# Trainium2: the first step of the later transforms on sums and differences of opposite rows, with 32x32 parts of the array

## The chip, the cores and the metric

One core of one Trainium2 chip. The core has TensorE (PE, 128x128 matmul array, with its weight loads shown apart as PEld), VectorE (DVE), ScalarE (ACT), GpSimd (POOL) and SyncE (SP), which mostly issues DMAs. Each engine works through its own queue in order and waits on semaphores of the others. The metric is the device time of one execution in microseconds (us), as the median of several.

## The reference

```python
X = np.fft.rfft(x, axis=1)                  # x: 8 batches, 3008 positions, 256 channels
F = (filt_r + 1j * filt_i)[None, :, :]      # one filter for all batches
y = np.fft.irfft(X * F, n=x.shape[1], axis=1)
x = y.reshape(8 * 3008, 256)                # 24064 tokens
g = x @ w_gate                              # 256 x 1536
return (g / (1 + np.exp(-g)) * (x @ w_val)) @ w_out     # 1536 x 256
```

All in float32. Along the positions each channel is filtered in the frequency domain; then each token goes through a gated feed-forward block (FFN).

## The kernel before

The FFN is most of the work. It runs batch by batch, and each batch in 12 steps (four chunks of tokens by three thirds of the hidden width). While batch b's FFN runs, the transform of batch b+1 is done in pieces between its products. The first transforms (batches 0 and 1) are done by other code. From the third batch on, that is during b = 1 to 6, the transform of batch b+1 has these pieces: in steps 0 to 3 its first step, `quads(0)` to `quads(3)`; in steps 4 to 10 `fours(...)`, which go on from the result; in step 11 nothing. In b = 7 there is nothing left to transform.

The order of all instructions is written out by hand: `SCHEDULE` is one list of tokens for a step, run through once per step, and `pin` keeps what is emitted in that order. A token names an operation of the FFN or a slot for transform work. `P`, `Q`, `A`, `B`, `E` with digits are products (`product`, L1075, 26 of them, two matmuls each), `W` and `o` the second matmuls of the FFN (L1172). The small letters before two digits are the operations around a product: `x03` makes an operand (L1097), `s13` another (L1097, written to the `wa` operand), which A13 multiplies; `c1` is a copy from PSUM by ScalarE (L1094), `y01`, `m13` and so on follow. `t` tokens call the transform's last step for other chunks. `b0` to `b7` each advance the step's iterator in `bursts` by one `yield`. The part of the order around them:

```python
"Q0 o3' z1.o' t4.2' W2 b0 f0 S00' S01' i0 b1 b2 x0.o' t0.0 x1.o' i1 Q1 t0.1 x2.o' P3 x3.o' f1 t4.3'"
"W1 x4.o' S10' x03 S11' D01 i2 i3 i4 s13 b3 x5.o' P1 o1 b4 t0.2 P0 o2 z0.o c1 i5 A13 g1 c0 S20' Q2"
...
" ... h2 b5 Q3 t2.1 h01 e12 A02 y23 W4 e02 b6 y03 m02 g3 ... l12 b7 E02 u12 ..."
```

**The first step before.** The 3008 positions are 47 rows (N1) of 64 (N2). `quads(g)` treats two pieces u = 2g and 2g+1, each of four neighbouring positions in each half of a row, 47 rows by 1024 numbers in each half of the partitions. At b0 eight matmuls (L716) multiply the 47 rows by a table of cosines and negated sines (47x64, the 48 outputs being 24 frequencies by real and imaginary part) on four 64x64 parts of the array. Each fp32 matmul is recorded as two passes. At b1 and b2, per piece, ScalarE copies one PSUM bank (L725), and VectorE subtracts and adds the other (L331 and L328, called from L726 and L727). At b3 and b4 ScalarE issues two stores each (L733) of 48 rows to the batch's `d1` tile in DRAM, and SyncE loads the x of a later piece (`load_x(u + 2)`, L618 as the helper's line). `load_four` (L743) reads `d1` back after step 3.

x is loaded into a shared SBUF tile `lent`, of which `room_of(name)` hands out places; a burst's tables, intermediate values and the filter's temporary share it. The x of the next batch's first two pieces is asked for in step 11, at Q2 and B01. In b = 1, steps 0 to 3, SyncE also carries the rearranging of the filter (`keep_filter` and `negated_filter`).

Of the kernel before, what the change touches and what calls it, by code (L numbers as in the profile page):

```python
# [41 lines left out]
FP32 = mybir.dt.float32  # L42
# [6 lines left out]
B, S, C = 8, 3008, 256  # L49
# [4 lines left out]
N1, N2 = 47, 64  # L54
NS, NQ = 24, 64
# [70 lines left out]
def dft_tables():  # L126
# [37 lines left out]
            if n >= NH:  # L164
                back[row:row + rows, first + N1 * i:first + N1 * (i + 1)] = one_hi[a:a + rows]

    quad = np.zeros((128, 64))
    for h, turn in enumerate((ph, ph + 2 * np.pi * s / (2 * N1))):
        cols = np.stack([np.cos(turn), -np.sin(turn)], 2).reshape(N1, 2 * NS)
        quad[64 * h:64 * h + N1, 0:2 * NS] = cols  # L170

    four = np.zeros((128, N_FOUR + 1, 2, 4, 64))
    lo, qq = np.arange(32), np.arange(32)
# [32 lines left out]
def kernel(  # L206
# [60 lines left out]
    def weights_of(b, k, g):  # L267
        return wt_1 if b == 0 and k < NT and g == 1 else wt_t

    dram_tiles = [wdpool.tile([2 * NS, N2, C], FP32, name=f"d{1 + i % 2}_{i // 2}")  # L270
                  for i in range(4)]
    yt_dram = [wdpool.tile([128, 3 * len(PAIRS), TQ], FP32, name=f"yt_{k}") for k in range(NT)]
    y_dram = [wdpool.tile([128, 8, TQ], FP32, name=f"y_{k}") for k in range(NCHUNK)]
    o_dram = [wdpool.tile([128, 4 * NH, RP], FP32, name=f"o_{k}") for k in range(NT)]
# [39 lines left out]

    def negated_filter(w, stage):

        t = room_of("et"[w % 2])[0:64].rearrange("p (s c) -> p s c", c=C)
        if stage == 0:
            for q in range(4):
                pin(nc.sync.dma_start(out=t[16 * q:16 * q + 16],  # L320
                                      in_=filter_rows(1, q // 2, q % 2, 4 * w, 4)))
        elif stage == 1:
            pin(nc.scalar.mul(t, t, -1.0))
        else:
            pin(nc.sync.dma_start(out=f_pairs[:, 0, 1, 4 * w:4 * w + 4], in_=t))
# [274 lines left out]
    class Spectral:  # L600


        def __init__(self, b):
            self.b = b
            self.d1, self.d2 = [dram_tiles[2 * (b % 2) + i] for i in range(2)]
# [23 lines left out]
        def load_x(self, u):  # L629
            if self.b == 0:  # L630
                rows = x[0].rearrange("(r n) c -> r n c", n=32)
                for a, n in ((0, 4), (4, 4)):
                    for r in (slice(0, 80), slice(80, NR)):
                        self.load(out=x0[u][r, a:a + n, :],
                                  in_=rows[r, 8 * u + a:8 * u + a + n, :])
            elif self.b > 1:
                if u < N_QUAD:
                    self.x[u] = room_of("x", u).rearrange("p (n c) -> p n c", c=C)
                    rows = x[self.b].rearrange("(r n) c -> r n c", n=N2)
                    for h in range(2):  # L640
                        for a, e in ((0, 32), (32, N1)):
                            self.load(out=self.x[u][64 * h + a:64 * h + e],
                                      in_=rows[a:e, 32 * h + 4 * u:32 * h + 4 * u + 4])
            elif u < N_ONE:
                self.x[u] = xpool.tile([NR, NV, C], FP32, name=f"x_{self.b}_{u}", tag="x")
                rows = x[self.b].rearrange("(r n) c -> r n c", n=32)

                for r in (slice(0, 80), slice(80, NR)):
                    self.load(out=self.x[u][r], in_=rows[r, ts(u, NV), :])
# [49 lines left out]
        def bank(self, name):  # L699
# [2 lines left out]
                return bank(name).rearrange("p (i c) -> p i c", i=NV)  # L702
            return fbank(name)

        def quads(self, g):

            pieces = (2 * g, 2 * g + 1)
            banks = {}
            for u in pieces:
                xt = self.x.pop(u)  # L710
                for h in range(2):
                    banks[u, h] = bank(f"qa_{self.b}_{u}_{h}")
                for cp in range(2):
                    for h in range(2):
                        r = slice(64 * h, 64 * h + N1)
                        pin(nc.tensor.matmul(  # L716
                            out=banks[u, h][64 * cp:64 * cp + 64], lhsT=quad_t[0][r, 0:64],
                            rhs=xt[r, 2 * cp:2 * cp + 2].rearrange("p n c -> p (n c)"),
                            start=True, stop=True))
            yield  # L720
            t1 = {u: room_of("yg"[i]).rearrange("p (n h c) -> p n h c", h=2, c=C)
                  for i, u in enumerate(pieces)}
            for u in pieces:
                low, high = [banks[u, h].rearrange("p (n c) -> p n c", c=C) for h in range(2)]
                pin(nc.scalar.copy(out=t1[u][:, :, 0], in_=low))  # L725
# [3 lines left out]
            d1 = self.d1.rearrange("a (n h) c -> a n h c", h=2)  # L729
            for u in pieces:  # L730
                for cp in range(2):
                    n = 4 * u + 2 * cp
                    pin(nc.scalar.dma_start(out=d1[:, n:n + 2], in_=t1[u][64 * cp:64 * cp + 2 * NS]))  # L733
                self.load_x(u + 2)
                yield
            if g == 3:
                self.load_filter(0)
                self.load_turns(0)
            yield
            if g == 3:  # L740
                self.load_four(0)

        def load_four(self, w):  # L743

            if w < N_FOUR:
                t = self.t2[w] = room_of("t").rearrange("p (s h c) -> p s h c", h=2, c=C)
                d1 = self.d1.rearrange("(s r) (n h) c -> s (r n) (h c)", r=2, h=2)
# [633 lines left out]
    for b in range(B):  # L1381
# [10 lines left out]
        if b and nxt:  # L1392
            for n in range(N_QUAD // 2):
                bursts[n] = nxt.quads(n)
            for n in range(N_FOUR + 1):
                bursts[N_QUAD // 2 + n] = nxt.fours(n)
        bursts = [iter(p) for p in bursts]
        two = []
        for u in range(N_TWO + 2) if b == 0 else ():
# [18 lines left out]
        for step in range(NCHUNK * NG + (b == B - 1)):  # L1418
# [16 lines left out]
            for place, token in enumerate(SCHEDULE):  # L1435
# [31 lines left out]
                    continue  # L1467
                if b == 0 and (step, op) == (5, "A23"):
                    nxt.load_two(0)
                if b + 2 < B and (step, op) in ((11, "Q2"), (11, "B01")):  # L1470
                    following.load_x(int(op == "B01"))
                if b == 1 and step < 4 and op in FILTER_AT:
                    n = FILTER_AT.index(op)
                    if n < 4 and step < 3:
# [48 lines left out]
```

## Time and profile before

| | us |
|---|---|
| median of 3 runs | 2821.73 |
| the runs | 2825.27, 2821.73, 2821.25 |
| the profiled execution | 2823.7 |
| its span, first to last instruction | 2821.6 |

The mean granted clock of TensorE over the span is 0.997 of full speed. The profile is of one execution, so sums made from its durations stand against 2823.7.

| group | busy, us |
|---|---|
| L1075 products, operand `wa` (x4464) | 881.6 |
| L1075 products, operand `wk` (x2976) | 572.0 |
| L1172 second matmuls, `wA` (x1532) | 551.8 |
| L1075 products, operand `we` (x2232) | 431.7 |

How to read it: "busy" of an engine is the sum of its instructions; matmuls are pipelined, so several can be in flight and a busy PE isn't one at its peak. "idle before" is time in which an engine stood before an instruction of the group, with what ended it. The chain of waits follows the work that ended last back to what released it. In names such as `wqa<-lent,quad` the output stands left of the arrow. DMA moved 586.59 MB in the span, 208 GB/s in the mean.

### The profile page before, as it was taken

Reading aid. Unit: us, or ns where it says so; the run is one execution under the profiler, and the core shown is the slowest. Engines: PE = TensorE matmul, PEld = TensorE weight load, DVE = VectorE, ACT = ScalarE, POOL = GpSimd, SP = SyncE. Lnnn points to the kernel's source line nnn. Section 1 sums busy time; section 2 is a strip of 40 time slices with the busy share of each in tenths; the row PEclk is TensorE's granted clock in tenths of the full one; section 3 lists DMA queues with packets and bytes.
Section 4 is the critical chain, followed back from the end, with each engine's and each line's share of the span. In section 5 each row is a group of like instructions: output and inputs, shape, how many; then the busy total and the mean of one; then the engine's idle time right before and its main releaser. Section 6 shows DMA issues by size and latency. Waiting matters only on the chain.

```text
span 2821.6 us, 48540 instructions
## 1 busy us (share of the span) xinstructions
PE 2787.5 (99%) x15444; PEld 2319.9 (82%) x15444; DVE 1999.1 (71%) x4579; ACT 1564.7 (55%) x4176; POOL 1579.9 (56%) x1689
## 2 busy tenths in 40 slices
PE   8999999999999999999999999999999999999998
PEld 6877888888888888788888888878888888888887
DVE  7898767767667766667766677667676767666666
ACT  5675455555555555555555555555555555555554
POOL 4786576465545565456653566445655455545544
PEclk9999999999999999999999999999999999999999
DMA  9687876877666775667666676667766677654443
GB/s 214 224 272 237 283 242 211 285 233 232 181 188 207 246 221 175 204 215 229 222 185 197 211 246 201 188 190 236 228 205 181 213 224 227 192 153 148 153 137 82
DMA packets 362933, 586.59 MB, mean 208 GB/s; under 512 B 198620, under 2 KB 245660, under 8 KB 362536
## 3 DMA queue, kind: packets, MB, share of 16 engines
q1 hardware_dynamic: 337722, 533.61, 60.8%
q10 hardware_dynamic: 22318, 44.38, 5.7%
q0 software_dynamic: 2640, 5.51, 0.7%
q8 instruction: 125, 2.05, 0.3%
q14 instruction: 128, 1.05, 0.1%
HBM read 467.48 MB, written 101.34 MB: 202 GB/s over the span
## 4 chain that ended last, share of the span: by engine, by line
PE 91%; POOL 2%; DVE 2%; DMA 1%; issue 1%; ACT 1%; ACTq 0%; SPq 0%; POOLq 0%; DVEq 0%
PE wa L1075 25%; PE wk L1075 17%; PE wA L1172 16%; PE we L1075 13%; PE wG L1172 8%; PE wF L1172 4%; PE pd L978 3%; PE wqa L716 2%; PE wqc L775 1%; PE wqb L787 1%; POOL out_dram L1157 0%; POOL h L331 0%; PE pa L857 0%; DMA lent<-later_tbl 0%; PE pd L981 0%
## 5 line engine op out<-in xcount | busy, mean ns | idle before, releaser
L1075 PE MATMUL wa<-y_t,wt_t 128*128 128x188 f32 x4464 | 881.6, 324 | 4.0 <-DVE wa L1097 2.3
L1075 PEld LDWEIGHTS wa<-y_t,wt_t 128*128 128x128 f32 x4464 | 749.8, 191 | 79.5 <-ACT wa L1101 9.3
L1075 PEld LDWEIGHTS wk<-y,wt_t 128*128 128x128 f32 x2976 | 495.0, 190 | 109.5 <-issue 33.4
L1075 PE MATMUL wk<-y,wt_t 128*128 128x188 f32 x2976 | 572.0, 325 | 3.2 <-ACT f L1090 3.2
L331 POOL TENSOR_TENSOR h<-h 128x376 f32<-128x376 f32 x572 | 559.6, 1000 | 15.4 <-DVE h L328 15.2
L328 POOL TENSOR_TENSOR h<-h 128x376 f32<-128x376 f32 x190 | 182.8, 983 | 685.5 <-DVE h L1122 685.5
L1172 PE MATMUL wA<-h,wo_t 128*128 128x376 f32 x1532 | 551.8, 482 | 3.9 <-DVE o L328 2.1
L1075 PE MATMUL we<-y_t,wt_t 128*128 128x188 f32 x2232 | 431.7, 323 | 1.6 <-ACT we L1106 1.5
L331 POOL TENSOR_TENSOR D<-f,f 128x376 f32<-128x376 f32 x288 | 280.0, 986 | 258.4 <-ACT f L1090 256.0
L331 DVE TENSOR_TENSOR we<-we,m 128x376 f32<-128x376 f32 x576 | 319.8, 556 | 141.1 <-PE we L1075 73.9
L1075 PEld LDWEIGHTS we<-y_t,wt_t 128*128 128x128 f32 x2232 | 369.3, 190 | 2.7 <-ACT we L1106 2.1
L1172 PEld LDWEIGHTS wA<-h,wo_t 128*128 128x128 f32 x1532 | 274.9, 190 | 113.7 <-issue 7.0
L1110 ACT COPY m<-wa 128x376 f32<-128x376 f32 x576 | 272.7, 473 | 102.0 <-PE wa L1075 98.8
L335 DVE SCALAR_TENSOR_TENSOR y<-wk,c 128x376 f32<-128x376 f32 x480 | 244.8, 541 | 63.8 <-ACT c L1094 37.8
L1117 ACT ACTIVATE g<-wa 128x188 f32<-128x188 f32 x576 | 187.5, 326 | 164.7 <-PE wa L1075 154.9
L1117 ACT ACTIVATE u<-we 128x188 f32<-128x188 f32 x576 | 188.7, 328 | 160.2 <-DVE we L331 153.3
L1172 PE MATMUL wG<-h,wo_t 128*128 128x376 f32 x768 | 274.0, 479 | 0.0
L1094 ACT COPY c<-wk 128x376 f32<-128x376 f32 x288 | 136.5, 474 | 226.0 <-PE wk L1075 196.7
L1090 ACT ACTIVATE f<-wk 128x376 f32<-128x376 f32 x288 | 140.4, 488 | 168.6 <-PE wk L1075 118.0
L1106 ACT COPY we<-y 128x376 f32<-128x376 f32 x480 | 222.3, 480 | 19.8 <-DVE h L1122 14.4
L1122 DVE TENSOR_TENSOR h<-wa,g 128x188 f32<-128x188 f32 x576 | 199.4, 347 | 38.0 <-ACT g L1117 37.6
L1122 DVE TENSOR_TENSOR h<-we,u 128x188 f32<-128x188 f32 x576 | 198.5, 345 | 28.8 <-ACT u L1117 17.3
(193 smaller groups left out, 3523.0 us busy)
## 6 DMA issues: line engine op xcount, KB each, us to landing
wt_t<-w_all SPq DMA_DIRECT2D x174, 896.0 KB
wt_t<-w_all SPq DMA_DIRECT2D x174, 768.0 KB
lent<-filter SPq DMA_DIRECT2D x36, 1024.0 KB
lent<-d SPq DMA_DIRECT2D x84, 256.0 KB
d<-lent ACTq DMA_DIRECT2D x84, 256.0 KB
d<-lent ACTq DMA_DIRECT2D x96, 192.0 KB
lent<-raw SPq DMA_DIRECT2D x144, 128.0 KB
t<-d SPq DMA_DIRECT2D x114, 128.0 KB
```

The source lines that it names most:

```text
L328: return eng.tensor_tensor(out=dst, in0=a, in1=b, op=ALU.add)
L331: return eng.tensor_tensor(out=dst, in0=a, in1=b, op=ALU.subtract)
L335: return nc.vector.scalar_tensor_tensor(out=dst, in0=a, scalar=-1.0, in1=b, op0=ALU.mult, op1=ALU.subtract)
L978: pin(nc.tensor.matmul(out=rows, lhsT=self.t4[k, i][:, j, ts(cb, 128)], rhs=cols, start=j == 0, stop=True, skip_group_check=True))
L1075: pin(nc.tensor.matmul(out=ps[:, z], lhsT=self.wt[:, SLOT[p], z], rhs=rhs, start=start and z == 0, stop=True, skip_group_check=True))
L1090: pin(act.mul(self.small(f"f{i}", f"f{i}", 1), t[f"k{i}"], -1.0))
L1094: pin(act.copy(out=self.small(f"c{i}", f"c{i}", 1), in_=t[f"k{i}"]))
L1106: pin(act.copy(out=self.bank(f"e{at}"), in_=t[f"y{at}"]))
L1110: pin(act.copy(out=self.small(f"m{at}", "m", 4), in_=t[f"a{at}"]))
L1117: pin(act.activation(out=self.small(op, "g", 3, 1)[:, 0], in_=ps[:, 1], func=AF.Silu))
L1122: pin(v.tensor_tensor(out=dst, in0=ps[:, 0], in1=g, op=ALU.mult))
L1172: pin(nc.tensor.matmul(out=self.tiles[at], lhsT=wo_t[:, JB * q + i, WO[p], :], rhs=self.hs[i][:, HID[p]], start=start and i == 0, stop=Tru ...
```

## The change

The row of the sum over 47 rows that lies at the same distance on the other side of the middle has the same cosine, and a sine of opposite sign. The change makes sums and differences of such opposite rows before the matmul, and multiplies the sums by cosines and the differences by sines alone, on 32x32 parts of the array. 47 rows become 24 sums and 24 differences, of which the middle row is met by itself (cosine halved, sine zero).

- New in every step that precedes a `quads`: `fold(g)`, four VectorE operations of 128x512 in SBUF, at b4, b5, b6 and b7, two sums into place `e` and two differences into place `t`. For the first step, `first_fold` does it in step 11 of the batch before.
- `quads(g)`: pieces g and g+4 instead of 2g and 2g+1; 16 matmuls of 24 rows by 32 columns by 512 instead of 8. Copies, subtractions and additions stay.
- Stores are of 64 rows instead of 48, to DRAM tiles of their own (`quads_dram`), and `load_four` reads these.
- x: six loads per fold (64, 23, 23, 2, 64 and 64 rows of 4 KB) instead of four per piece; a batch has 24 instead of 32. They are issued after the last operation of the fold before (b7), and for the first fold at Q0 of step 11.
- The temporary of `negated_filter` moves to the last two places of the shared tile.

Lines of the changed kernel lie 35 to 41 further down around the transform's code.

```diff
-    quad = np.zeros((128, 64))
-    for h, turn in enumerate((ph, ph + 2 * np.pi * s / (2 * N1))):
-        cols = np.stack([np.cos(turn), -np.sin(turn)], 2).reshape(N1, 2 * NS)
-        quad[64 * h:64 * h + N1, 0:2 * NS] = cols
+    quad = np.zeros((4, 32, 2, 32))
+    for h in range(2):
+        turn = 2 * np.pi * (np.outer(2 * np.abs(23 - 23 * h - n1[0:NS]) + h, s) % (2 * N1)) / (2 * N1)
+        quad[2 * h:2 * h + 2, 0:NS, 0, 0:NS], quad[2 * h:2 * h + 2, 0:NS, 1, 0:NS] = np.cos(turn), -np.sin(turn)
+        quad[2 * h:2 * h + 2, 23] *= np.array([0.5, 0.0])[:, None]
+    quad = quad.reshape(128, 64)
...
+    quads_dram = [wdpool.tile([64, N2, C], FP32, name=f"quads_{i}") for i in range(2)]
...
-        t = room_of("et"[w % 2])[0:64].rearrange("p (s c) -> p s c", c=C)
+        t = lent[64 * (w % 2):64 * (w % 2) + 64, 12 * NV * C:14 * NV * C]
+        t = t.rearrange("p (s c) -> p s c", c=C)
...
-                if u < N_QUAD:
-                    self.x[u] = room_of("x", u).rearrange("p (n c) -> p n c", c=C)
-                    rows = x[self.b].rearrange("(r n) c -> r n c", n=N2)
-                    for h in range(2):
-                        for a, e in ((0, 32), (32, N1)):
-                            self.load(out=self.x[u][64 * h + a:64 * h + e],
-                                      in_=rows[a:e, 32 * h + 4 * u:32 * h + 4 * u + 4])
+                if u < N_QUAD // 2:
+                    self.x[u] = [room_of("x", n) for n in range(2)]
+                    up, down = self.x[u]
...
+                    self.load(out=up[0:64], in_=rows(0, NS - 1, -1, ("i", 2), ("p", 32)))
+                    for i in range(2):
+                        self.load(out=down[32 * i:32 * i + NS - 1],
+                                  in_=rows(0, NS, 1, ("p", NS - 1), i=i))
+                    self.load(out=down[NS - 1:64:32], in_=rows(0, 0, 1, ("i", 2)))
+                    self.load(out=up[64:128], in_=rows(1, 0, 1, ("i", 2), ("p", 32)))
+                    self.load(out=down[64:128], in_=rows(1, N1 - 1, -1, ("i", 2), ("p", 32)))
...
+        def fold(self, g):
+
+            if g < N_QUAD // 2:
+                up, down = self.x.pop(g)
+                self.x[g] = [room_of("e"), room_of("t")]
+                for t, f in zip(self.x[g], (add, sub)):
+                    for half in range(2):
+                        a = ts(half, NV * C)
+                        pin(f(nc.vector, t[:, a], up[:, a], down[:, a]))
+                        if t is self.x[g][1] and half:
+                            self.load_x(g + 1)
+                        yield
+
+        def first_fold(self):
+
+            for _ in range(4):
+                yield
+            yield from self.fold(0)
...
-            pieces = (2 * g, 2 * g + 1)
-            banks = {}
-            for u in pieces:
-                xt = self.x.pop(u)
-                for h in range(2):
-                    banks[u, h] = bank(f"qa_{self.b}_{u}_{h}")
-                for cp in range(2):
-                    for h in range(2):
-                        r = slice(64 * h, 64 * h + N1)
-                        pin(nc.tensor.matmul(
-                            out=banks[u, h][64 * cp:64 * cp + 64], lhsT=quad_t[0][r, 0:64],
-                            rhs=xt[r, 2 * cp:2 * cp + 2].rearrange("p n c -> p (n c)"),
-                            start=True, stop=True))
-            yield
+            pieces = (g, g + N_QUAD // 2)
+            banks = {(u, h): bank(f"qa_{self.b}_{u}_{h}") for u in pieces for h in range(2)}
+            parts = self.x.pop(g)
+            for cp in range(2):
+                for t in range(2):
+                    for i, u in enumerate(pieces):
+                        for h in range(2):
+                            r, c = 32 * (2 * h + i), 32 * (2 * cp + t)
+                            pin(nc.tensor.matmul(
+                                out=banks[u, h][c:c + 32], lhsT=quad_t[0][r:r + NS, ts(t, 32)],
+                                rhs=parts[t][r:r + NS, ts(cp, NV * C)],
+                                start=True, stop=True))
+            yield
+            fold = self.fold(g + 1)
...
-                    pin(nc.scalar.dma_start(out=d1[:, n:n + 2], in_=t1[u][64 * cp:64 * cp + 2 * NS]))
-                self.load_x(u + 2)
+                    pin(nc.scalar.dma_start(out=d1[:, :, n:n + 2], in_=t1[u][64 * cp:64 * cp + 64]))
+                if u == pieces[1]:
+                    next(fold, None)
                 yield
             if g == 3:
                 self.load_filter(0)
                 self.load_turns(0)
+            next(fold, None)
             yield
             if g == 3:
                 self.load_four(0)
+            next(fold, None)
+            yield
+            next(fold, None)
...
+        if b + 2 < B:
+            bursts[-1] = following.first_fold()
...
-                if b + 2 < B and (step, op) in ((11, "Q2"), (11, "B01")):
-                    following.load_x(int(op == "B01"))
+                if b + 2 < B and (step, op) == (11, "Q0"):
+                    following.load_x(0)
```

More of the change, by code (lines that the diff above doesn't have):

```diff
@@ L604, in __init__ @@
             self.b = b
+            self.quads_dram = quads_dram[b % 2]
             self.d1, self.d2 = [dram_tiles[2 * (b % 2) + i] for i in range(2)]
@@ L636, in load_x, with rows @@
             elif self.b > 1:
-                if u < N_QUAD:
-                    self.x[u] = room_of("x", u).rearrange("p (n c) -> p n c", c=C)
-                    rows = x[self.b].rearrange("(r n) c -> r n c", n=N2)
-                    for h in range(2):
-                        for a, e in ((0, 32), (32, N1)):
-                            self.load(out=self.x[u][64 * h + a:64 * h + e],
-                                      in_=rows[a:e, 32 * h + 4 * u:32 * h + 4 * u + 4])
+                if u < N_QUAD // 2:
+                    self.x[u] = [room_of("x", n) for n in range(2)]
+                    up, down = self.x[u]
+                    xb = x[self.b]
+                    def rows(h, first, step, *dims, i=0):
+                        at = (N2 * first + 32 * h + 4 * u + 16 * i) * C
+                        ap = [[{"i": 16, "p": step * N2}[d] * C, n] for d, n in dims]
+                        return bass.AP(tensor=xb.tensor, offset=xb.offset + at,
+                                       ap=ap + [[1, 4 * C]])
+                    self.load(out=up[0:64], in_=rows(0, NS - 1, -1, ("i", 2), ("p", 32)))
[5 more added lines that the diff above has]
+                    self.load(out=down[64:128], in_=rows(1, N1 - 1, -1, ("i", 2), ("p", 32)))
             elif u < N_ONE:
@@ L728, in quads @@
                 yield
-            d1 = self.d1.rearrange("a (n h) c -> a n h c", h=2)
+            d1 = self.quads_dram.rearrange("(s t) (n h) c -> t s n (h c)", t=2, h=2)
             for u in pieces:
@@ L746, in load_four @@
                 t = self.t2[w] = room_of("t").rearrange("p (s h c) -> p s h c", h=2, c=C)
-                d1 = self.d1.rearrange("(s r) (n h) c -> s (r n) (h c)", r=2, h=2)
+                d1 = self.quads_dram.rearrange("(s r) (n h) c -> s (r n) (h c)", r=2, h=2)
                 for p in range(2):
```

## The prediction

> **What bounds the kernel now.** I read the page's busy times and chain first, then the groups by line, then one step's timeline. All in microseconds.
>
> ```profile
> PE 2787.5 (99%) x15444; PEld 2319.9 (82%) x15444; DVE 1999.1 (71%) x4579; ACT 1564.7 (55%) x4176; POOL 1579.9 (56%) x1689
> ...
> PE 91%; POOL 2%; DVE 2%; DMA 1%; issue 1%; ACT 1%; ACTq 0%; SPq 0%; POOLq 0%; DVEq 0%
> ```
>
> TensorE (PE) sets the end. A microsecond taken from it is worth a microsecond only where its next work is ready; the other engines have room on average, so only their lateness at one place can count. The rows of the burst that changes, and (last) the nearest row for the operation that is added, columns busy, mean ns of one, idle before:
>
> ```profile
> L716 PE MATMUL wqa<-lent,quad 47*64 47x512 f32 x384 | 46.7, 602 | 0.0
> ...
> L328 DVE TENSOR_TENSOR lent<-lent,wqa 128x512 f32<-128x512 f32 x48 | 33.0, 687 | 1.7
> L331 DVE TENSOR_TENSOR lent<-lent,wqa 128x512 f32<-128x512 f32 x48 | 32.8, 684 | 68.4 <-ACT lent L725 62.4 <-DMA t<-d 6.0
> ...
> L725 ACT COPY lent<-wqa 128x512 f32<-128x512 f32 x48 | 28.1, 586 | 47.0 <-PE wqa L716 47.0
> ...
> L845 DVE TENSOR_TENSOR lent<-lent 128x512 f32<-128x512 f32 x24 | 16.4, 683 | 0.0
> ```
>
> 384 recorded matmul passes in 24 bursts (six batches, steps 0 to 3) are 46.7 us, 1.95 each. What such a burst costs comes from step lengths, taken between the first product of consecutive steps: step 2 is 27.61 with a burst and 25.40 in the last batch, which has none. So a burst costs 2.21, about 53 us in all. In the timeline of TensorE around 449.5 the rounds start at 449.57, 450.05, 450.48 and 450.90, the next product at 451.44: four rounds of 0.43 (1.71) and some 0.5 of switching.
>
> Then what waits for the burst, in step 1 of batch 3 (start, length, engine, line):
>
> ```profile
> 1159.76 1.95 PE L716 MATMUL wqa<-lent,quad 47*64 47x512 f32 x16
> ...
> 1160.90 0.59 ACT L725 COPY lent<-wqa 128x512 f32<-128x512 f32 x1 [1.75 <-PE wqa L716]
> 1161.52 0.69 DVE L331 TENSOR_TENSOR lent<-lent,wqa 128x512 f32<-128x512 f32 x1 [2.39 <-ACT lent L725]
> ...
> 1164.62 0.55 DVE L1097 SCALAR_TENSOR_TENSOR wa<-wk,f 128x376 f32<-128x376 f32 x1
> ...
> 1165.52 0.67 PEld L1075 LDWEIGHTS wa<-y_t,wt_t 128*128 128x128 f32 x4
> 1165.68 0.80 PE L1075 MATMUL wa<-y_t,wt_t 128*128 128x188 f32 x4
> ```
>
> VectorE stands idle for 2.39 until the first copy, does four operations of some 0.69 in a row, then x03 and s13 (L1097). s13 ends at 1165.17 and the weights of its product A13 load at 1165.52, 0.35 later. So A13 is 0.35 away from waiting on this chain, which starts at the burst and not at the step's start.
>
> The windows of that batch (length, PE, PEld, DVE, ACT, POOL busy) for steps 0 and 1:
>
> ```profile
> 1128.60:1157.80 29.20, 29.20 (x162) 23.88 (x161) 21.43 (x49) 15.38 (x42) 12.31 (x15) 1.00 0.64 198
> 1157.80:1187.00 29.20, 29.20 (x162) 23.88 (x161) 18.88 (x44) 16.45 (x43) 10.64 (x13) 1.00 0.71 198
> ```
>
> VectorE has 7.8 free in the fuller of them. Last, from what waits on the stores of the burst (L733):
>
> ```profile
> ACT c L1094: 22.1, 10
> ```
>
> Ten times ScalarE was held at a store for 2.2 each: a store that can't be issued stops ScalarE's own work behind it. And of the landing times that the list of DMA issues has (KB, median from issue to landing), the nearest in size to a burst's store and to a load:
>
> ```profile
> d<-x POOLq DMA_DIRECT2D x2, 256.0 KB, 3.7
> ...
> t<-d POOLq DMA_DIRECT2D x2, 256.0 KB, 4.9
> ```
>
> **What the Trainium skill says.** "TensorEngine Tiling (Array Packing)", Key Properties: tiles load and multiply independently, and changing the tiling mode drains the array. The trace agrees for four parts: within a round they start about 7 ns apart, and about 0.5 per burst lies outside the rounds. "TensorE: Matmul & The Clock Gate", Measured speedup vs the span model: sixteen 32x32 tiles of 512 columns ran 10.6 times as fast as one after another. No run here shows sixteen, nor the two passes of fp32 on them. "TensorEngine Tiling (Array Packing)", PSUM Bottleneck: tiling doesn't speed up the evacuation of PSUM; the chain above is that evacuation. "DMA: Bandwidth & Descriptors", Anatomy of one DMA: a wait of a DMA is made on the issuing sequencer before dispatch; the held ScalarE above agrees.
>
> **The change, part by part.**
>
> *TensorE.* 8 matmuls on four parts become 16 on sixteen, each two passes. If all parts run at once, four rounds become two: 2 × 0.43 = 0.85 less. Switching stays 0.5. Bounds: 16 parts in groups of eight take four rounds (nothing gained), in groups of four eight rounds (4 × 0.43 = 1.7 more). I take two rounds.
>
> *What of that counts.* The copies and the four VectorE operations have the size that they had, so A13 can start at most 0.35 earlier relative to the burst's start, and 0.1 more if its weight load (0.16 ahead of its matmul above) runs less far ahead. Against this, in the kernel before the first piece's banks were complete after two rounds and its copy began before the burst had ended (1160.90 against 1161.71); now all banks end together, after two rounds and a spread of starts, some 0.1 later. So 0.85 is cut to about 0.3 a burst; the remaining 0.5 turns into a wait at A13. Bounds: 0.85 (VectorE reordered, nothing late) and 0.
>
> *VectorE.* 4 sums and differences of 128x512 in each of 24 folds: 96 × 0.683 = 65.6, or 2.73 a step. The two steps above have 7.8 and 10.3 free. They stand at b4 to b7, in slots after A13's operands are made, so in order they push what follows by 0.68 to 1.4 for a short time. The y and h operations behind them in the page have stretches of idle (L335 DVE: 63.8 over 480). I cost them at nothing where x is there; cover gone, 0.68 each, 65 at most.
>
> *ScalarE.* Two copies and four stores, as before; stores of 64 rows for 48 (a third more bytes, 16 KB x 4 more a burst). Nothing.
>
> *SyncE and x.* 32 loads of x per batch become 24 (from 3.0 to 3.8 MB), issued together after the last fold (b7) and not in pairs after the stores. From b7 to the next step's b4 is about half a step, some 14, three times the 4.9 of a load. So x is there in time, unless a load is held. Here the built order of the changed kernel decides: each DMA of SyncE and ScalarE takes one of eight completion semaphores in turn, and waits until the DMA that had it eight places before has landed. In batch 1, where SyncE also carries the loads and stores of the filter, the last loads of x in steps 1 and 2 come to wait for a store of that same step's burst. Those stores are issued 3.2 to 4.9 after the burst starts (1162.96 and 1164.67 against 1159.76), land 3.7 later, and then the load needs 4 to 5 of its own: x at 11 to 13 after the burst, while VectorE reaches b4 at about 5.5. It stands there for 5 to 7, and behind it in its queue are s01, y01 and m13, whose products come a few microseconds later. TensorE has 2 to 3 of other work ready. I take 4 for each of these two steps, +8; bounds 0 (x early enough) and 14.
>
> *A store that waits for a store.* In step 2 of the other five batches the fourth store of a burst gets the semaphore of the first of the same burst, issued about 1.7 earlier. Landing after 3.7, it holds ScalarE about 2, the size of the waits in the fence above. Behind it is the copy c (L1094), whose y and product follow. I take 0.9 instead of −0.3 there: 5 × 0.9 = +4.5; bounds −1.5 and +10.
>
> *Edits with one answer.* The table in new blocks and the halved rows: no time. Filter's temporary elsewhere in the shared tile: nothing, its places are free in those steps. Step 11's first fold: VectorE has 10 free there, its x is asked at the step's start.
>
> *Sum.* 24 bursts less 5 (store) less 2 (x) are 17 at −0.3: −5.1; +4.5; +8. That is +7.4. The profiled execution of 2823.7 (span 2821.6, 2 around it) becomes 2831.1; it is 2.0 above the median of the runs, so the prediction is **2829**. A change under 0.2% (5.6) can't be told from none by this measurement.
>
> **The rivals.**
> 1. *Wash.* Loads and stores land faster than I take (3 rather than 4 to 5), so the holds are half: −5.1 + 5 × 0.3 + 3, about −1: 2821. For it: in the kernel before only one burst row (L331, 6.0 of 68.4) shows a wait for a DMA. Against it: the built order puts the waits there. 0.24, with most of it within 0.2%.
> 2. *Parts don't all overlap.* In groups of eight nothing is gained: +12 to +20, 2834 to 2842. In groups of four each burst is 1.7 longer: 41 + 12 to 20, about 2878. For: sixteen are shown nowhere here; against: the four parts of before overlap fully and the skill's measurement. 0.10 and 0.05.
> 3. *Faster: the cap isn't there.* The other side, one mechanism: A13 isn't held, since the weight load of A13 doesn't stand for what s13 allows, or the first copy starts earlier because the burst is over sooner. Then 0.85 × 24 = −20.4, and even with +12 of holds −8: 2801 to 2814. It decides once more than 0.65 a burst is gained. Against: s13 ends 0.35 before the load now, and the chain doesn't shrink. 0.10.
> 4. *VectorE is the bound.* It goes to 2065 of 2822, and in step 0 to 24.2 of 29.2; as an average no bound. If each fold costs its 0.68 once per step: 24 × 0.68 = +16, 2845. 0.05, inside the range.
>
> **How the numbers follow.** Forecast 0.46, rivals as given. Range: from a wash with holds gone (−5) to holds at their upper bounds or groups of eight or a visible fold (+28), 2817 to 2850; below and above are left 0.10 and 0.09. Slower by over 0.2%: forecast 0.42, wash 0.04, parts 0.15, VectorE 0.05, 0.66 in all; within 0.2%: 0.04 + 0.18 + 0.01 of the faster case, 0.23; faster 0.11.
>
> **What would show it.** Right: bursts of about 1.2 in place of 1.95; A13 (wa, L1075) with a new idle of about 0.5 released by VectorE; two steps of batch 1 longer by some 4, with VectorE waiting there for x; ScalarE held at the fourth store in step 2. Wrong: bursts of 1.95 or more; step lengths 0.85 shorter in steps 0 to 3; no wait of the folds for a DMA; VectorE late in steps that have x in time.

## The result and the profile after

| | kernel before | changed kernel |
|---|---|---|
| median, us | 2822.18 (4 runs) | 3538.26 (4 runs, 3535.6 to 3539.82) |
| ratio, 95% interval | | 1.2534 (1.2512 to 1.2556) |
| profiled execution, us | 2823.7 | 3539.82 (span 3538.0) |
| mean granted TensorE clock | 0.997 | 0.904 |

The changed kernel is 716 us slower; 2829 was predicted, 2850 was the upper end. The mechanism is in two lists, the page of the changed kernel and its waits. First the page: busy times, then groups (busy, mean ns of one, idle before).

```profile
PE 2876.2 (81%) x15828; PEld 2379.3 (67%) x15828; DVE 2054.1 (58%) x4675; ACT 1555.9 (44%) x4176; POOL 1580.4 (45%) x1689
...
L1134 ACT COPY c<-wk 128x376 f32<-128x376 f32 x288 | 136.4, 474 | 595.1 <-DMA quads<-lent 264.0 <-PE wk L1115 182.3 <-DMA out_dram<-o 82.2
...
L332 DVE TENSOR_TENSOR lent<-lent 128x512 f32<-128x512 f32 (+1 forms) x51 | 34.9, 685 | 491.7 <-DMA lent<-in_x_dram 438.0 <-DMA out_dram<-o 20.9 <-DMA quads<-lent 20.6
...
L750 PE MATMUL wqa<-lent,quad 24*32 24x512 f32 x768 | 27.4, 600 | 0.0
```

TensorE does about what it did, in a longer span. Its burst became shorter: 27.4 over 24 bursts is 1.14 each, against 1.95, so all sixteen parts do overlap. VectorE now stands 438 us in front of the fold's operations for x, and ScalarE 264 us behind stores of the burst that can't be issued. The chain of waits, in one stretch of the last batch that has a burst (start, length, what):

```profile
2881.09 34.45 DMA lent<-in_x_dram
2915.61 0.49 ACTq L768
...
2940.43 1.36 PE wqa L750 x32
2946.65 27.54 DMA quads<-lent
2974.34 3.82 DMA lent<-quads
```

(The chain can be followed back over the last fifth of the span only, so its shares by engine say little here.) A load of x takes 34 us from issue to landing and a store of the burst 28, where the prediction took 4 to 5 and 3.7. (They are the last of a fold's six loads and the last of a burst's four stores, so each time holds the DMAs ahead of it too.) The second line shows a link that matters below: ScalarE's third store of that burst is issued 0.07 us after the load of x has landed. The windows of the same kernel tell why the DMAs are slow. The last three columns are the granted clock, the mean busy share of the 16 DMA engines, and the GB/s that they moved:

```profile
2883.00:2892.00 9.00, 9.00 (x72) 6.52 (x72) 4.79 (x11) 3.97 (x11) 4.08 (x5) 1.00 0.13 51
...
2901.00:2907.00 6.00, 0.00 (x0) 0.00 (x0) 0.00 (x0) 0.00 (x0) 0.00 (x0) 0.60 0.13 53
...
2905.00:2910.00 5.00, 0.00 (x0) 0.00 (x0) 0.00 (x0) 0.00 (x0) 0.00 (x0) 0.50 0.17 64
...
2958.00:2964.00 6.00, 6.00 (x36) 5.50 (x35) 4.72 (x13) 3.87 (x12) 0.00 (x0) 1.00 0.14 55
2964.00:2970.00 6.00, 6.00 (x32) 4.88 (x30) 4.85 (x12) 2.73 (x8) 2.10 (x3) 1.00 0.13 53
```

The first row has loads of x alone, the last has stores of the burst alone, and the second has both. In all three the DMA engines are 0.13 busy: two of sixteen are 0.125. They move 51 to 53 GB/s, some 26 each. That loads and stores together keep no more engines busy than either alone says that they are on the same two. In the kernel before, the steps shown ahead have shares of 0.64 and 0.71 at 198 GB/s. In the third row no engine computes at all, and TensorE's clock is granted at 0.50; the first products after the wait then run slower: in that chain four `wk` passes take 1.62 us from 2918.79, right after the wait, and 0.64 from 2924.75. The wait itself, in VectorE's timeline, stands where b4 was put, with everything of TensorE's operands behind it:

```profile
2894.40 0.54 DVE L332 TENSOR_TENSOR o<-o,wA 128x376 f32<-128x376 f32 x1
2915.66 0.69 DVE L332 TENSOR_TENSOR lent<-lent 128x512 f32<-128x512 f32 x1 [20.72 <-DMA lent<-in_x_dram]
2916.27 0.54 DVE L332 TENSOR_TENSOR o<-o,wF 128x376 f32<-128x376 f32 x1
```

The time lies in few steps. The table has lengths in us between the first products of consecutive steps, median over batches 2 to 6 (step 11: 1 to 5), and the sum of what all steps of the profiled execution lie above the kernel before; the experiments are explained below:

| kernel | step 0 | 1 | 2 | 3 | 4 | 11 | sum | of it batch 1 |
|---|---|---|---|---|---|---|---|---|
| before | 29.21 | 29.21 | 27.61 | 27.60 | 29.82 | 28.60 | | |
| changed | 52.20 | 63.48 | 51.42 | 29.82 | 41.29 | 51.04 | +717 | 139 |
| e1_x_spread | 39.75 | 36.59 | 36.45 | 31.61 | 40.58 | 29.35 | +286 | 75 |
| e2_stores_spread | 48.72 | 47.50 | 43.45 | 27.68 | 29.82 | 50.65 | +458 | 84 |
| e3_both_spread | 30.07 | 28.99 | 27.88 | 27.68 | 29.83 | 30.20 | +35 | 22 |
| e5_repaired | 32.00 | 28.99 | 28.35 | 27.68 | 29.83 | 33.93 | +65 | 21 |
| e7_late_folds | 34.95 | 28.99 | 29.20 | 27.69 | 29.82 | 28.60 | +48 | 14 |
| e12_stores_by_sync | 29.36 | 28.48 | 27.80 | 27.15 | 29.82 | 28.60 | −5 | 0 |

Step 11 has loads of x and no store, step 3 stores and no loads, step 4 the reading of what step 3 stored: both sides of the change are in it.

### The profile page after: what moved, and what is told of

The parts are those of the page before. It is cut to its first block, busy times and chain, and to the rows that moved or that the text cites. A ratio compares the mean times of both kernels' runs of the same rounds, so it can differ in the third digit from the quotient of the medians.

```text
span 3538.0 us, 49230 instructions
## 1 busy us (share of the span) xinstructions
PE 2876.2 (81%) x15828; PEld 2379.3 (67%) x15828; DVE 2054.1 (58%) x4675; ACT 1555.9 (44%) x4176; POOL 1580.4 (45%) x1689
## 5 line engine op out<-in xcount | busy, mean ns | idle before, releaser
L1115 PE MATMUL wa<-y_t,wt_t 128*128 128x188 f32 x4464 | 914.5, 333 | 194.5 <-DVE wa L1137 187.5
L1115 PEld LDWEIGHTS wa<-y_t,wt_t 128*128 128x128 f32 x4464 | 777.3, 197 | 281.2 <-DVE wa L1137 190.8
L1115 PE MATMUL wk<-y,wt_t 128*128 128x188 f32 x2976 | 597.0, 334 | 350.2 <-ACT f L1130 347.7
L1115 PEld LDWEIGHTS wk<-y,wt_t 128*128 128x128 f32 x2976 | 507.5, 195 | 473.2 <-ACT f L1130 364.7
L1212 PE MATMUL wA<-h,wo_t 128*128 128x376 f32 x1532 | 574.1, 498 | 53.0 <-ACT o L1224 49.2
L1212 PEld LDWEIGHTS wA<-h,wo_t 128*128 128x128 f32 x1532 | 289.5, 199 | 167.4 <-issue 66.1
L332 DVE TENSOR_TENSOR lent<-lent 128x512 f32<-128x512 f32 (+1 forms) x51 | 34.9, 685 | 491.7 <-DMA lent<-in_x_dram 438.0
```

Source lines behind the costliest of these rows:

```text
L332: return eng.tensor_tensor(out=dst, in0=a, in1=b, op=ALU.add)
L1115: pin(nc.tensor.matmul(out=ps[:, z], lhsT=self.wt[:, SLOT[p], z], rhs=rhs, start=start and z == 0, stop=True, skip_group_check=True))
L1212: pin(nc.tensor.matmul(out=self.tiles[at], lhsT=wo_t[:, JB * q + i, WO[p], :], rhs=self.hs[i][:, HID[p]], start=start and i == 0, stop=Tru ...
```

## The experiments

Three theories stood at the start. A: a DMA whose pattern has an outer dimension of two rows is worked by two DMA engines, and one of 23 rows by one. B: rows in descending order are slow. C: the shared completion semaphores hold the DMAs, whatever their shape.

**The x loads by one step over 64 rows** (e1_x_spread).

```diff
-                    self.load(out=up[0:64], in_=rows(0, NS - 1, -1, ("i", 2), ("p", 32)))
+                    self.load(out=up[0:64], in_=rows(0, 0, 1, ("i", 64)))
...
-                        self.load(out=down[32 * i:32 * i + NS - 1],
-                                  in_=rows(0, NS, 1, ("p", NS - 1), i=i))
+                        for p, n in ((0, 16), (16, NS - 17)):
+                            self.load(out=down[32 * i + p:32 * i + p + n],
+                                      in_=rows(0, NS + p, 1, ("p", n), i=i))
...
-                    self.load(out=up[64:128], in_=rows(1, 0, 1, ("i", 2), ("p", 32)))
-                    self.load(out=down[64:128], in_=rows(1, N1 - 1, -1, ("i", 2), ("p", 32)))
+                    self.load(out=up[64:128], in_=rows(0, 0, 1, ("i", 64)))
+                    self.load(out=down[64:128], in_=rows(0, 0, 1, ("i", 64)))
```

> The changed kernel with its three 64-row loads of x written with one step over 64 rows (so they read other rows of x: the output differs) and each 23-row load split into 16 and 7; bytes, row size and everything else stay. Theory A (a DMA whose outer dimension has 2 rows is worked by 2 of the 16 DMA engines, 23 rows by 1): x lands in some 4 us, VectorE's 438 us of waiting for x go, step 11 falls from 51 to 29 us; what stays are the stores on 2 engines, about 20 us per burst, which hold steps 3 and 4: 2880 to 3050 us. Theory B (a row order that descends is slow): the same gain in x, but nothing left at the stores: about 2830. Theory C (the eight completion semaphores in turn hold the loads, whatever their shape): no large change, 3400 to 3600.

Measured 3105.04, ratio 1.1008 (1.0976 to 1.104). The waiting for x fell from 438 to 65 us, step 11 from 51 to 29. The time is 55 us above the upper end of A's range, so the stores cost more by themselves than A had it; B and C are far off.

**Ascending instead of descending** (e1b_ascending).

```diff
-                    self.load(out=up[0:64], in_=rows(0, NS - 1, -1, ("i", 2), ("p", 32)))
+                    self.load(out=up[0:64], in_=rows(0, 0, 1, ("i", 2), ("p", 32)))
...
-                    self.load(out=down[64:128], in_=rows(1, N1 - 1, -1, ("i", 2), ("p", 32)))
+                    self.load(out=down[64:128], in_=rows(1, N1 - 32, 1, ("i", 2), ("p", 32)))
```

> The changed kernel with the two descending loads of x made ascending, still as 2 outer rows by 32 (other rows of x are read, so the output differs). Theory A (two outer rows, two DMA engines): no change, 3500 to 3580. Theory B (descending order is slow): most of the 438 us of waiting for x go, 2950 to 3150.

Measured 3540.79, ratio 1.2552 (1.2516 to 1.2589), as the changed kernel. The direction costs nothing; B falls.

**The stores as 64 plain rows** (e2_stores_spread).

```diff
-            d1 = self.quads_dram.rearrange("(s t) (n h) c -> t s n (h c)", t=2, h=2)
+            d1 = self.quads_dram.rearrange("r (n h) c -> r n (h c)", h=2)
...
-                    pin(nc.scalar.dma_start(out=d1[:, :, n:n + 2], in_=t1[u][64 * cp:64 * cp + 64]))
+                    pin(nc.scalar.dma_start(out=d1[:, n:n + 2], in_=t1[u][64 * cp:64 * cp + 64]))
...
```

> The changed kernel with the stores of the burst written as 64 plain rows to a tile laid out as real part, then imaginary part; the reads of that tile become two of 32 rows each instead of one of 64. Same bytes, right output. Theory A: the stores land in some 4 us and ScalarE's 264 us of waiting for them go; step 4 falls from 41 to 30, step 11 stays at 51 since x is still on few engines: 3150 to 3350 us. Theory B (descending x): the stores were never slow, no change. Theory C (semaphores in turn): about no change.

Measured 3277.78, ratio 1.162 (1.1586 to 1.1654). Steps 3 and 4 are back at 27.68 and 29.82, step 11 is at 51 as foreseen. ScalarE's waiting fell to 108 us only, not to none. The semaphores in the traces show why. Each DMA of SyncE and ScalarE takes one of eight completion semaphores, and it is issued only when the last DMA that had the same semaphore has landed. Here 26 of the 96 stores are issued within 0.1 us of the landing of a load of x, 22 within 0.1 us of that of another DMA, and none waits for a store. In the changed kernel it is 27, 23 and none. So much of ScalarE's 264 us came from slow x, handed on by a semaphore; with fast x (e1_x_spread) they fell to 73.

**Two outer rows put into the kernel before** (e4_before_stores_2).

```diff
-            d1 = self.d1.rearrange("a (n h) c -> a n h c", h=2)
+            d1 = padded[self.b % 2].rearrange("(a r) (n h) c -> a r n (h c)", a=2, h=2)
...
-                    pin(nc.scalar.dma_start(out=d1[:, n:n + 2], in_=t1[u][64 * cp:64 * cp + 2 * NS]))
+                    pin(nc.scalar.dma_start(out=d1[:, 0:NS, n:n + 2],
+                                            in_=t1[u][64 * cp:64 * cp + 2 * NS]))
...
```

> The kernel before, with only its burst stores changed: the 48 rows go to a padded tile as 2 outer rows by 24 instead of 48 by one step; same bytes, same number of DMAs. Theory A: 384 KB per burst on each of two engines at the 26 GB/s each that the changed kernel's trace shows (53 over two) are 15 us, so stores land 10 to 15 us later, ScalarE waits at them, and steps 0 to 4 grow: 2860 to 2960 us. Theories B and C: 2822.

Measured 2945.48, ratio 1.0442 (1.0412 to 1.0472). Nothing of the change is in this kernel but the shape of a store, and it loses 125 us. C falls with it as the cause, since number and order of the DMAs are the old ones; the semaphores only hand a delay on. The place was not quite the one expected: ScalarE hardly waits for these stores, and step 4, which reads them, has the largest loss of the later batches (35.45 against 29.82).

**Both repairs together** (e3_both_spread: the edits of e1_x_spread and e2_stores_spread), and **with the right rows** (e5_repaired).

```diff
-        turn = 2 * np.pi * (np.outer(2 * np.abs(23 - 23 * h - n1[0:NS]) + h, s) % (2 * N1)) / (2 * N1)
+        turn = 2 * np.pi * (np.outer(2 * np.abs(23 - n1[0:NS]) + h, s) % (2 * N1)) / (2 * N1)
...
-                    self.load(out=up[0:64], in_=rows(0, NS - 1, -1, ("i", 2), ("p", 32)))
+                    self.load(out=up, in_=rows(0, NS - 1, -1, ("i", 4), ("p", 32)))
...
+                        self.load(out=down[at:at + NS], in_=rows(1, NS - 1, 1, ("p", NS), i=i))
```

> The changed kernel with both repairs (x loads of 64 rows by one step, which read other rows of x, so the output differs; stores of 64 plain rows): every large DMA of the change is on 16 engines, and nothing else is altered. If the few DMA engines were the whole of the loss, what is left is the prediction's own sum: bursts of 1.36 us, no wait for x or stores above 4 us, 2815 to 2840 us. If something else in the change is slow too (VectorE's folds, 32x32 parts), 2850 or more.

> The same with the right rows: the table takes both halves' rows as 23-p, so all descending rows are one load of 4 outer rows by 32 (4 engines, 128 KB each, some 5 us at 26 GB/s), the ascending ones are loads of 24, 16 and 7 rows; stores as in e2_stores_spread. Eight loads a fold instead of six. Theory A: like e3_both_spread within 10 us, 2815 to 2850, and no fold waits longer than some us for x except in step 11, where x is asked for about 6 us before it is used. If four engines are still too few: over 2880.

Measured 2856.49, ratio 1.0122 (1.0108 to 1.0136), and 2889.03, ratio 1.0239 (1.0225 to 1.0253). So 680 of 716 us go with the shape of the DMAs when other rows of x are read, and some 650 with the right rows. What is left in e3_both_spread lies above the prediction's range, and the step lengths name its places: batch 1, where steps 1 and 2 are 39.56 and 36.94 against 29.07 and 27.47, step 11, and step 0. With four engines for the descending rows x comes later still, and step 11 grows to 34; e5_repaired is in the range that was set for too few engines.

In step 3 of e3_both_spread nothing waits for x, and no store waits for a semaphore. It shows the burst and what follows from it:

```profile
1244.66 1.14 PE L751 MATMUL wqa<-lent,quad 24*32 24x512 f32 x32
...
1246.07 1.07 ACT L761 COPY lent<-wqa 128x512 f32<-128x512 f32 x2 [2.02 <-PE wqa L751]
...
1249.79 0.55 DVE L1140 SCALAR_TENSOR_TENSOR wa<-wk,f 128x376 f32<-128x376 f32 x1
...
1250.49 0.88 PE L1118 MATMUL wa<-y_t,wt_t 128*128 128x188 f32 x4 [0.34 <-POOL h L335]
```

The last row is A13. Its operand s13, in the row above, ends at 1250.34; TensorE stands 0.34 before A13. (The view names GpSimd as the releaser; e8_late_reordered below shows that it is VectorE's order that counts.)

**Folds of 16 columns** (e6_folds_small).

```diff
                         a = ts(half, NV * C)
+                        a = slice(a.start, a.start + 16)
                         pin(f(nc.vector, t[:, a], up[:, a], down[:, a]))
```

> e5_repaired with each fold operation cut from 512 to 16 columns (the output differs): order, count, waits and DMAs stay, VectorE's time for the folds falls from 0.68 to about 0.1 us each. If the folds' length is hidden, as the prediction took it, the same time as e5_repaired within 3 us; if each of them shows by 0.5 us or more, 12 to 50 us less.

Measured 2883.85, ratio 1.0223 (1.0209 to 1.0237), 5 us less than e5_repaired, and the two intervals overlap. Steps 1 and 3 are the same to 0.01, so a fold's length is hidden where x is there. In step 11, where the folds wait for x, the median is 2.2 shorter (31.69 against 33.93): there the length may come on top of the wait.

**Folds at b5 to b7** (e7_late_folds).

```diff
-            for _ in range(4):
-                yield
-            yield from self.fold(0)
+            fold = self.fold(0)
+            for n in (0, 0, 0, 0, 0, 1, 1, 2):
+                for _ in range(n):
+                    next(fold, None)
+                yield
...
-                if u == pieces[1]:
-                    next(fold, None)
...
             next(fold, None)
+            next(fold, None)
```

> e5_repaired with the four fold operations of a step at b5, b6, b7 and b7 instead of b4 to b7, so that x has some 7 us more to land; nothing else altered, right output. If what is left in e5_repaired (69 us over the kernel before) is x that comes after b4 (step 11, and steps 0 to 2 of batch 1), most of it goes: 2818 to 2835, step 11 at 28.6 again, steps 1 and 2 of batch 1 below 31. If it is the DMA engines' load or the stores, over 2860.

Measured 2865.12, ratio 1.0151 (1.0132 to 1.017). Step 11 is at 28.60 and step 1 of batch 1 at 30.86, so x was late there and no longer is. But the whole stayed above the expectation, because step 0 grew to 34.95. From the list of waits (total, times, longest):

```profile
ACT c L1139 <- DMA quads<-lent: 38.6, 6, 7.1
```

All six are in step 0. The trace shows there, in each batch, that the fourth store takes the semaphore of the first store of the same burst and is issued 0.02 us after that one has landed.

**VectorE reordered** (e8_late_reordered): the second piece's two operations move from b2 to b3, behind x03 and s13.

```diff
-                pin(sub(nc.vector, t1[u][:, :, 1], t1[u][:, :, 0], high))
-                pin(add(nc.vector, t1[u][:, :, 0], t1[u][:, :, 0], high))
-                yield
...
+            evacuate(pieces[1], True)
+            yield
+            evacuate(pieces[1], False)
+            store(pieces[0])
...
```

> e7_late_folds with the second piece's subtraction and addition moved behind x03 and s13 on VectorE (from slot b2 to b3). If those four operations are what holds A13 after the shorter burst (in e3_both_spread s13 ended 0.11 before A13's weight load, and TensorE stood 0.34), each of 24 bursts gains 0.3 to 0.5 us: 7 to 12 us less than e7_late_folds. If something else holds TensorE there: no change within 3 us, or more where the PSUM banks come free later.

Measured 2867.8, ratio 1.0162 (1.0148 to 1.0176): no gain. The timeline of its step 3 shows that the reordering did what it should, and what took the gain (burst first):

```profile
1243.00 1.14 PE L754 MATMUL wqa<-lent,quad 24*32 24x512 f32 x32
...
1246.47 3.34 ACTq L775 DMA_DIRECT2D quads<-lent  x4
...
1248.33 0.80 PE L1133 MATMUL wa<-y_t,wt_t 128*128 128x188 f32 x4
...
1249.86 0.47 ACT L1152 COPY c<-wk 128x376 f32<-128x376 f32 x1 [3.98 <-PE wk L1133]
```

A13 comes 5.33 after the burst's start, against 5.83 in e3_both_spread. But ScalarE stands 3.98 before its copy c; the view names a product as its releaser, but the four stores lie between, and the third of them waits until 1248.70 for VectorE's second piece. The copy and what follows from it are late, and step 3 became 28.20.

**The stores later** (e9_stores_at_b5, e9a_stores_at_b6).

```diff
             evacuate(pieces[1], False)
-            store(pieces[0])
-            yield
-            store(pieces[1])
+            yield
             yield
+            store(pieces[0])
+            store(pieces[1])
...
```

> e8_late_reordered with all four stores of a burst at b5, behind ScalarE's copies c1 and c0, and step 3's read of them at b7. In e7_late_folds and e8_late_reordered the fourth store of step 0 takes the completion semaphore of the first of the same burst (the built order shows it), ScalarE stands 6 to 7 us there, and step 0 is 35 us instead of 29. Here no store waits for one of its own burst in steps 0 to 2, and ScalarE's copies are ahead of the stores. If these two are what is left: step 0 at 28.9 or less, steps 1 to 3 0.3 to 0.5 below those of the kernel before, 2805 to 2822 us. If TensorE stands for another reason: 2835 or more.

> e9_stores_at_b5 with the stores one slot later, at b6; in step 3 of each batch the fourth store still waits for the second, in both. If ScalarE has room at both places: within 3 us of e9_stores_at_b5. If a held store hurts less at b6: up to 10 us less.

Measured 2866.77, ratio 1.0161 (1.0147 to 1.0174), and 2838.45, ratio 1.0057 (1.0044 to 1.007). Step 0 did come down (31.04 and 29.54), but at b5 ScalarE was held before other work: 31.7 us before L1164 and 13.3 before L1051. In step 2 of batches 2 to 6 a store still waited for the first of its own burst, against what was expected. At b6 the kernel is 28 us faster than at b5, more than either expectation allowed, with 17.2 us before L1168. So the place of a store chooses whom it holds, and for how long.

**The stores by SyncE** (e12_stores_by_sync).

```diff
-                    pin(nc.scalar.dma_start(out=d1[:, n:n + 2], in_=t1[u][64 * cp:64 * cp + 64]))
+                    pin(nc.sync.dma_start(out=d1[:, n:n + 2], in_=t1[u][64 * cp:64 * cp + 64]))
```

> e9_stores_at_b5 with the four stores issued by SyncE instead of ScalarE, same slot. If ScalarE held at a store (31.7 us before L1164 and 13.3 before L1051 in e9_stores_at_b5) is what keeps the steps with a burst long, these waits go, steps 0 and 1 fall to 29 or less and steps 2 and 3 to 27.2: 2808 to 2824 us, at or below the kernel before. If TensorE waits for something else there: over 2840.

Measured 2817.17 (14 runs) against 2821.26, ratio 0.9983 (0.9975 to 0.9991). It is 4 us below the kernel before, a small gain whose interval stays below 1, and 50 us below e9_stores_at_b5. No wait for a store is left in its list of the engines' waits; of waits for x one of 3.1 us. Its step 3:

```profile
1215.19 1.14 PE L754 MATMUL wqa<-lent,quad 24*32 24x512 f32 x32
...
1219.01 0.55 DVE L1155 SCALAR_TENSOR_TENSOR wa<-wk,f 128x376 f32<-128x376 f32 x1
...
1220.08 0.47 ACT L1152 COPY c<-wk 128x376 f32<-128x376 f32 x1 [2.02 <-PE wk L1133]
...
1220.52 0.80 PE L1133 MATMUL wa<-y_t,wt_t 128*128 128x188 f32 x4
```

A13 is 5.33 after the burst, s13 is done 0.96 before it, and the copy c is in time. Step 3 is 27.15, 0.45 below the kernel before, of the 0.81 by which the burst is shorter; step 1 is 0.73 below, step 0 and step 2 are 0.15 and 0.19 above, where the expectation had both below. The kernel before was not run with its stores on SyncE, so how much of the 4 us such a move alone would bring there is open.

## Why the prediction was wrong

**The step that failed** is "SyncE and x", where it says "three times the 4.9 of a load. So x is there in time", and with it, under ScalarE, "stores of 64 rows for 48 (a third more bytes, 16 KB x 4 more a burst). Nothing." (16 rows of 4 KB are 64 KB a store; but the bytes were not what mattered.) Both price the new DMAs by the landing time of old ones of the same bytes. The change's own lines show the new shape (`("i", 2), ("p", 32)` for x, `t=2` for the stores), and the step did not price it. In the place of 4.9 the run had 34.45, in that of 3.7 it had 27.54. e1_x_spread, e2_stores_spread and e4_before_stores_2 show that the shape does it: 680 of the 716 us stood at nothing. The direction, slower, was forecast, but from 8 and 4.5 us of other waits. Those waits exist (e3_both_spread is still 36 us above the kernel before), but they are about a twentieth of the loss; that the direction came true says little for the sum.

A count of the busiest engine would have shown it. By A three loads of 256 KB lie on two engines and two of 92 KB on one, so one engine carries 3 × 128 + 2 × 92, with 4 more of the two-row load 572 KB, which at 26.5 GB/s are 22 us; the stores, 4 × 256 KB on two engines, are 512 KB or 20 us. That is 42 us in a step of 28, beside that engine's share of all else (0.64 to 0.71 of 29.2 us). The Trainium skill states the rule: "DMA: Bandwidth & Descriptors", Rules for kernel authors, says that an outermost dimension of size c below 16 confines a DMA to at most c engines, and its section Why a DMA increments its semaphore by 16 and not by 1 gives the number of engines as the largest up to 16 that divides both patterns' outer sizes. The shares of 0.13 here agree for two. The semaphore updates in the traces agree for every shape of the burst's loads and stores: a DMA of 64 or of 48 rows raises its semaphore in 16 steps, one of 2 × 32 rows in 3, one of 23 rows in 2, and in e5_repaired one of 4 × 32 rows in 5. Below 16 engines that is always one step more than the engines that this rule gives. The trace doesn't name the engines; that they are the same two is read from the windows above.

**Point by point.**
- *TensorE.* 1.14 a burst instead of 1.95; 0.81 less where 0.85 was taken, and all sixteen parts at once. This was right.
- *What of that counts.* The mechanism was right, the term a little large. In e3_both_spread's step 3 the first copy starts 1.41 after the burst's start, against 1.14 before (0.27 later where 0.1 was taken), and A13 5.83 against 5.93. TensorE stands 0.34 before A13 where about 0.5 was foreseen. Step 3 is 27.68 against 27.60 and step 1 is 28.99 against 29.21: instead of 0.3 a burst there is 0.2 or nothing. That the chain on VectorE is the cap is shown by e8_late_reordered and e12_stores_by_sync, where A13 comes at 5.33.
- *VectorE.* The folds' length is hidden where x is there, as e6_folds_small shows.
- *ScalarE.* "Ten times ScalarE was held at a store for 2.2 each" misread the list. In the kernel before no store waits for a semaphore: the last DMA that had it landed at least 0.46 us earlier in all 96 cases. At 1133.79 to 1136.08, one of the ten, 1.7 us are the issuing of four stores, and 0.4 a wait for VectorE's second piece. Stores that are held by a semaphore came with the change.
- *x in batch 1.* Two steps, each +4, were foreseen; in e3_both_spread, with loads at full speed, they are 10.5 and 9.5. The place was right, and so was the mechanism: the traces of the changed kernel and of e3_both_spread show loads of x there that wait for a store of the same step. The size was more than twice the term, and above its bound of 14 for both. The folds wait 10.0 and 7.4 there, where 5 to 7 was taken, and the steps lose at least as much, where TensorE was taken to have 2 to 3 of other work ready.
- *Step 11.* "VectorE has 10 free there, its x is asked at the step's start" looked at VectorE's room and not at the time from Q0 to b4. With loads at full speed it cost up to 1.6 in batches 1 to 5 and 4.0 in batch 0, with four engines about 5 in batches 1 to 5.
- *A store that waits for a store.* In the changed kernel it doesn't show: the fourth store of step 2 does take the first one's semaphore, but it comes so late, behind a third store that waits for x, that the first has landed long before. It shows in e3_both_spread, which has more loads a fold, in step 0 and not in step 2. There ScalarE stands 4.1 us before the copy c in each of batches 2 to 6, and the step is 0.86 longer. The size was met (0.9), the place was not.
- *The rivals.* None held the case: all took a DMA's landing time as given. Rival 2 doubted the parts of the array, which did as hoped; no rival doubted the DMAs' shape.

It was not tried why e12_stores_by_sync still loses 0.15 and 0.19 in steps 0 and 2, nor what each of its edits brings by itself: they were only added one after another.

## What to carry to other kernels

Price a DMA by its pattern and not by its bytes: where the outer dimension is small (here 2, 4 and 23 were run), work out the engines that it gets, divide the bytes by them, and add the busiest engine up over a step. Ask too which DMA had its semaphore before, since a slow DMA holds the next user of its semaphore on any queue. Keep stores off the queue of an engine whose work others wait for, since a store that waits stops all that is behind it; moving them took 50 us off here. And before a shorter burst is counted as a gain, find the chain that starts at it; here step 3 gained nothing until that chain was reordered and the stores were out of ScalarE's way.

## What was not expected of the hardware

- A row pattern of two by 24 in place of 48, for 96 stores of 192 KB, cost 125 us (e4_before_stores_2), with no byte more.
- In long waits TensorE's granted clock fell to 0.50. The mean rose as the waits went: 0.904 in the changed kernel, 0.96 in e1_x_spread, 0.993 in e3_both_spread.
- A DMA on few engines shows in its semaphore: 3 updates for 2 × 32 rows and 2 for 23, against 16 for 64 rows (all loads and stores of the burst in the changed kernel, e1_x_spread and e5_repaired).
- Sixteen 32x32 parts with two fp32 passes each ran their 32 passes in 1.14 us, where one pass takes 0.60. They are two rounds of sixteen, which start 0.46 us apart in e12_stores_by_sync.
